# Decode attention with a gated feed-forward: one load of wo's blocks 20 to 25 in place of two, the join ahead of their rows, and ten semaphore presets on GpSimd instead of VectorE

## The chip, the cores and the metric

The kernel runs on one core of one Trainium2 chip. A core has five engines with programs of their own: TensorE (PE, with its weight loads as PEld), VectorE (DVE), ScalarE (ACT), GpSimd (POOL) and SyncE (SP), which here only issues DMA transfers. They wait for each other on semaphores. The metric is the device time of one execution in microseconds (us); lower is better. The profile is of one execution.

## The reference

One token x (512 values) goes through two branches that a scalar gate mixes. Branch A is attention with 32 query heads of 128 over a cache of 8 groups with 32,768 keys and values each; branch B is a SwiGLU feed-forward of width 1,792. All inputs are bf16.

```python
x = A_x                                              # (1, 1, 512)
g = sigmoid((x * gate_w).sum(-1, keepdims=True))
q = (x @ wq).reshape(B, Sq, 32, 128).transpose(0, 2, 1, 3)
k = repeat(k_cache, 4, axis=1); v = repeat(v_cache, 4, axis=1)   # caches (1, 8, 32768, 128)
p = softmax(einsum("bhqd,bhkd->bhqk", q, k) * 128 ** -0.5)
o = einsum("bhqk,bhkd->bhqd", p, v)
a = o.transpose(0, 2, 1, 3).reshape(B, Sq, 4096) @ wo            # wo (4096, 512)
b = (silu(x @ w_gate) * (x @ w_up)) @ w_down                     # w_down (1792, 512)
return g * a + (1 - g) * b
```

## The kernel before

The work is a stream of weights and cache through three pages of SBUF of 8 MB each (one row of 32,768 bf16 values a partition). Pages 0 and 1 take the keys of the eight groups in turn, page 2 the values, and before them wq, w_gate and w_up. Page 0 at last holds w_down and wo. All large loads stand in SP's program in one order: wq, x, gate_w, w_gate, w_up, the keys of group 0, then keys of group j+1 and values of group j by turns; a load waits on a semaphore until the page it overwrites has been read (`load_k`, L327, waits for transposes counted in `sem_tr`; `load_v`, L338, for matmuls counted in `sem_v_done`). At the end come w_down (L361), the values of the last group in three pieces (L369 to L372, each waiting for the part of the page it overwrites) and wo in six pieces (`load_wo`, L364 to L374), which wait for nothing of their own.

DVE transposes the keys piece by piece (L707), PE multiplies them with the queries (L445), DVE takes the maximum (L716), GpSimd spreads it over the partitions (L308), ACT takes exponentials (L567) and copies them into the place where PE reads them (L580), and PE multiplies them with the values (L472) and transposes the sums (L486). The loop over the groups is a real loop on PE (L534), ACT (L557) and DVE (L756).

So that the first pass needs no special case, ten semaphores get a value at the start (L605 to L611): `sem_sc`, two of `sem_v7`, `sem_v6`, `sem_k7`, `sem_acc`, `sem_red`, `sem_ep`, `sem_v` and `sem_tr`. In DVE's program these stand behind five memsets and ahead of the copy of x (L614). GpSimd's program at the start sets constants (L289 to L300), raises `sem_const` (L301) and waits for `sem_dve_gpart`, the gate's partial sums, which it adds up over the partitions (L303).

At the end the attention output (4,096 values as 32 columns `O2` of 128) meets wo, which lies as 32 blocks of 128 rows: partition p holds 32 consecutive rows of wo, 1 KB each, and block j is row j of every partition. `WO_CUTS` cuts the 32 blocks into loads, each with a semaphore of its own in `sem_wo`:

```python
WO_CUTS = [0, 16, 20, 24, 26, 30, 32]
KW = 2
KL = 4
```

The first `KW` = 2 loads (blocks 0 to 19) are multiplied in wide form (L513 to L524): a matmul per block with 512 columns, the blocks spread over four rows of `ps_w`, which already holds the feed-forward's part. DVE copies `ps_w` to `part` (L753). The rest goes in narrow form: `emit_rows` makes four matmuls of 128 columns each for a block (one for each quarter of the 512 outputs, each in a strip of 32 rows of `ps_c`), and `emit_wo(pe, k)` does so for each block of load k after a wait for `sem_wo[k]`. The join (L529) is `emit_rows` with `part` in fp32: it adds the four rows of `part` into `ps_c`. It waits for DVE's copy (`sem_dve_w`, L528).

`emit_wide` does in this order: the wide blocks; `emit_wo` of load 2 (blocks 20 to 23, L527), after a wait for `sem_dve_oz`, the spread-out copy of `O2`; the join; `emit_wo` of the loads 3 to `KL` - 1, here load 3 (blocks 24 and 25, L531). There the block "main" ends, with a barrier of all engines (L267). Behind the barrier PE does the loads from `KL` on (blocks 26 to 29, then 30 and 31), DVE casts `ps_c` to `res_row` (L767), and SP and ACT store one half each.

Of the kernel before, what the change touches and what calls it, by code (L numbers as in the profile page):

```python
# [14 lines left out]
def bass_gated_mix__gqa_block_cached__swiglu_ffn__decode_kernel(  # L15
# [31 lines left out]
    UNITS = RB // RPU  # L47
    SLOTS = 2
# [7 lines left out]
    assert S % 128 == 0 and NT == 256 and G == 8 and RB * NS * 4 == 4096  # L56
    assert KC * H * DH + 2 * KC * F <= PAGE and (FC + WOJ) * NOUT <= PAGE

    WO_CUTS = [0, 16, 20, 24, 26, 30, 32]
    KW = 2  # L60
    KL = 4
    WIDE = WO_CUTS[KW]
    RQ = 4
    NSTRIP = 4
# [12 lines left out]
    assert RQ * HPG <= 32 and RQ * DH == 512 and FC % 2 == 0  # L77
    assert WO_CUTS[-1] == WOJ and FC % 2 == 0

# [7 lines left out]
    with ExitStack() as es:  # L87
        def S_(name):
            return es.enter_context(nc.semaphore(name))
# [7 lines left out]
        sem_k7 = S_("s_k7")  # L97
        sem_v6 = S_("s_v6")
        sem_v = S_("s_v")
        sem_v7 = [sem_v] + [S_(f"s_v7{i}") for i in range(1, len(V7_CUTS) - 1)]  # L100
        sem_ld_wd = S_("s_ld_wd")
        sem_wo = [S_(f"s_wo{i}") for i in range(len(WO_CUTS) - 1)]
        sem_tr = S_("s_tr")
        sem_sc = S_("s_sc")
# [29 lines left out]
        sem_acc = S_("s_acc")  # L134
        sem_red = S_("s_red")
        sem_oc = S_("s_oc")
        sem_exp = S_("s_exp")
        sem_ep = S_("s_ep")
# [97 lines left out]
        def emit_rows(pe, lhs, rhs, last):  # L236
            for oc in range(OC):
                e = oc % RPS
                ins = pe.matmul(  # L239
                    ps_c[32 * oc : 32 * oc + (1 if e else SW), 0:128],  # L240
                    lhs(e),
                    rhs[:, oc * 128 : (oc + 1) * 128],
                    start=False,
                    stop=last,
                    skip_group_check=True,
                )
            return ins

        def emit_wo(pe, k):
            pe.wait_ge(sem_wo[k], 16)  # L250
            for j in range(WO_CUTS[k], WO_CUTS[k + 1]):
                ins = emit_rows(
                    pe,
                    lambda e: O2[:, j : j + 1] if e else O2z[:, j - WIDE, :],
                    wo_v[:, j, :],
                    j == WOJ - 1,
                )
            return ins
# [8 lines left out]
        with nc.Block("main") as block:  # L267
            @block.gpsimd
            def _(pool):
                npool = [0]  # L270

                def chain(ins):
                    ins.then_inc(sem_pool, 1)
                    npool[0] += 1
                    pool.wait_ge(sem_pool, npool[0])

                def ones_where(t, base, pattern):
                    return pool.affine_select(
                        out=t,
                        in_=t,  # L280
                        compare_op=ALU.not_equal,
                        fill=1.0,
                        base=base,
                        pattern=pattern,
                        channel_multiplier=1,
                    )

                pool.load_library(library_config.all_libraries[1])
                chain(pool.memset(eye2[:, :], 0.0))  # L289
                ones_where(eye2[:, :], 0, [[-1, 2]]).then_inc(sem_eye, 1)  # L290
                pool.memset(qblk[:, :], 0.0)
                pool.memset(spread, 0.0)
                pool.memset(ident_f[:, :], 0.0)
                pool.memset(selz[:, :], 0.0)
                chain(pool.memset(pmat[:, :], 0.0))
                ones_where(spread, 0, [[-32, NSTRIP], [0, NQ], [-1, QP]]).then_inc(sem_const, 1)
                ones_where(ident_f[:, :], 0, [[-1, 128]]).then_inc(sem_const, 1)
                ones_where(pmat[:, :], 0, [[-1, 32], [-32, 4]]).then_inc(sem_const, 1)
                for c in range(NSTRIP):
                    chain(ones_where(selz[:, SW - 1 : SW], -32 * c, [[0, 1]]))  # L300
                pool.sem_inc(sem_const, 1)  # L301
                pool.wait_ge(sem_dve_gpart, 1)
                pool.partition_all_reduce(gtot[:, :], gpart[:, :], 128, ReduceOp.add).then_inc(  # L303
                    sem_gtot, 1
                )
                for j in range(G):
                    pool.wait_ge(sem_pmax, j + 1)
                    pool.partition_all_reduce(  # L308
                        gmax[:, :], pmax[:, :], 128, ReduceOp.max
                    ).then_inc(sem_gmax, 1)  # L310
                pool.wait_ge(sem_exp, HPG * (G + 2))
                chain(pool.memset(O2z, 0.0))
                pool.partition_all_reduce(ssum[:, :], esum[:, :], 128, ReduceOp.add).then_inc(
                    sem_S, 1
                )

            @block.sync
            def _(sp):
# [45 lines left out]
                def load_wo(k):  # L364
                    a, b = WO_CUTS[k], WO_CUTS[k + 1]
                    src = A_wo.rearrange("(p j) n -> p j n", j=WOJ)
                    sp.dma_start(wo_v[:, a:b, :], src[:, a:b, :]).then_inc(sem_wo[k], 16)  # L367
# [9 lines left out]
            def _(pe):  # L377
# [129 lines left out]
                def emit_wide():  # L507
                    pe.wait_ge(sem_dve_oT2, 1)
                    pe.matmul(
                        ps_m[:, M_O0 : M_O0 + WOJ], pmat[:, :], O2a[:, :], start=True, stop=True  # L510
                    ).then_inc(sem_pe_O2, 1)
                    pe.wait_ge(sem_dve_O2, 1)
                    for k in range(KW):  # L513
                        pe.wait_ge(sem_wo[k], 16)
                        for j in range(WO_CUTS[k], WO_CUTS[k + 1]):
                            c = j % NSTRIP
                            ins = pe.matmul(
                                ps_w[32 * c : 32 * c + 1, :],
                                O2[:, j : j + 1],
                                wo_v[:, j, :],  # L520
                                start=False,
                                stop=False,
                                skip_group_check=True,
                            )  # L524
                    ins.then_inc(sem_pe_w, 1)
                    pe.wait_ge(sem_dve_oz, 1)
                    emit_wo(pe, KW)  # L527
                    pe.wait_ge(sem_dve_w, 1)  # L528
                    emit_rows(pe, lambda e: selz[:, SW - 1 : SW] if e else selz[:, :], part, False)  # L529
                    for k in range(KW + 1, KL):  # L530
                        emit_wo(pe, k)  # L531

                emit_q()
                with hinted(pe, "groups", 1, G + 3) as (p, arm):  # L534
                    arm()
                    with pe.If(((p + (G - 3)) >> 3) == 1):
                        emit_v(p - 1)
                        emit_reduce(p)
                    with pe.If(p < G + 1):
                        emit_s(p)  # L540
                    with pe.Else():
                        with pe.If(p == G + 1):
                            emit_wd()
                        with pe.Else():
                            emit_wide()
# [46 lines left out]
            def _(dve):  # L592
# [9 lines left out]
                dve.memset(ps_c[:, :], 0.0).then_inc(sem_psw, 1)  # L602
                dve.memset(ps_w[:, :], 0.0).then_inc(sem_psw, 1)
                dve.memset(ps_o[:, :], 0.0).then_inc(sem_v_done, VTURN)
                dve.sem_inc(sem_sc, SLOTS)  # L605
                for sem in sem_v7[1:] + [sem_v6, sem_k7, sem_acc]:
                    dve.sem_inc(sem, 1)
                dve.sem_inc(sem_red, 2)
                dve.sem_inc(sem_ep, 1)
                dve.sem_inc(sem_v, 16)  # L610
                dve.sem_inc(sem_tr, UNITS)  # L611
                xg = ps_m[:, M_X0 : M_X0 + 2 * KC].rearrange("p (c e) -> p e c", e=2)
                dve.wait_ge(sem_pe_x, 1)
                dve.tensor_copy(xT[:, :], xg[:, 0, :]).then_inc(sem_dve_x, 1)  # L614
# [147 lines left out]
        pe, dve = nc.tensor, nc.vector  # L762
        for k in range(KL, len(sem_wo)):
            ins = emit_wo(pe, k)
# [35 lines left out]
```

## Time and profile before

| what | value |
|---|---|
| time, median of 3 runs | 349.60 us (349.52 to 349.61) |
| time of the profiled execution | 349.47 us |
| its span (first to last instruction) | 347.9 us |
| granted TensorE clock, mean of the span | 0.619 |
| PE busy | 181.4 us, 52% |
| DVE busy | 191.2 us, 55% |
| ACT busy | 92.9 us, 27% |
| POOL busy | 8.4 us, 2% |
| bytes by DMA | 148.13 MB in 4,477 packets, mean 426 GB/s |

The page has the busy time of each engine, the span in 40 equal slices (a digit is the busy share in tenths), the DMA queues with the share of 16 DMA engines' time that their packets took, and the chain of waits that ended last. In that chain DMA holds 59% of the span, PE 18% and DVE 15%. A stretch of the chain that is put to DVE and PE in turn lies beside transfers that are still running, so a share of the chain is not by itself what an engine costs. The trace beneath the page holds every packet, every instruction and every semaphore record with its time; where a time is given to a hundredth of a microsecond below, it is from there.

### The profile page before, as it was taken

The page shows a single profiled execution, that of the slowest core. Times are in us where ns is not written, and L with a number is a line of the kernel's source. Part 1 is how long each engine was busy: PE and PEld are TensorE (multiplying, and loading weights), DVE is VectorE, ACT ScalarE, POOL GpSimd, SP SyncE. Part 2 cuts the span into 40 slices and gives each one's busy share as a digit, 9 for nine tenths or more (in the row PEclk, how much of TensorE's full clock was granted, in tenths as well). Part 3 has the DMA queues.
Part 4 walks back from the last instruction along what each step waited for, and adds up shares of the span by engine and source line. Part 5 has one row for each costly group of instructions (what it writes and reads, how often), then busy time and mean ns, then how long its engine had stood idle before and what let it go on. Part 6 is the DMA issues. An engine that isn't in the chain of part 4 may idle for free.

```text
span 347.9 us, 7702 instructions
## 1 busy us (share of the span) xinstructions
PE 181.4 (52%) x2755; PEld 110.9 (32%) x2755; DVE 191.2 (55%) x311; ACT 92.9 (27%) x220; POOL 8.4 (2%) x29
## 2 busy tenths in 40 slices
PE   0393553556426570556235570556245575567555
PEld 0141442443124420443124420443034334431112
DVE  4024996996059911995069802994079839920001
ACT  1002002902640057003810057003810075038000
POOL 4000000000000000000000000000000000010000
PEclk9998555555855566555855567555855585558655
DMA  8999999989899898998989989899898999999996
GB/s 332 415 460 422 482 392 452 482 362 482 362 482 482 362 482 362 482 482 362 482 362 482 482 362 482 362 482 475 369 482 362 422 463 441 422 407 467 392 428 268
DMA packets 4477, 148.13 MB, mean 426 GB/s; under 512 B 506, under 2 KB 508, under 8 KB 1148
## 3 DMA queue, kind: packets, MB, share of 16 engines
q1 hardware_dynamic: 4472, 148.12, 98.9%
q8 instruction: 1, 0.02, 0.0%
q10 hardware_dynamic: 4, 0.00, 0.0%
HBM read 148.11 MB, written 0.00 MB: 426 GB/s over the span
## 4 chain that ended last, share of the span: by engine, by line
DMA 59%; PE 18%; DVE 15%; issue 7%; SPq 1%; DVEq 0%
DMA page<-in_A_k_cache_dram 39%; DVE slot L707 13%; DMA page<-in_A_wo_dram 8%; DMA page<-in_A_v_cache_dram 8%; PE ps_sc L445 7%; PE ps_o L472 5%; PE ps_sc L400 4%; DMA E<-in_gate_w_dram 3%; SPq L367 0%; SPq L320 0%; DVE qblk L637 0%; PE ps_c L239 0%; DVE E L654 0%; DVE oT L695 0%; DVE E L663 0%
## 5 line engine op out<-in xcount | busy, mean ns | idle before, releaser
L707 DVE STREAM_TRANSPOSE slot<-page 128x512 f32<-128x512 f32 x256 | 167.0, 690 | 91.2 <-DMA page<-in_A_k_cache_dram 81.1
L445 PE MATMUL ps_sc<-qcur,slot 128*128 128x16 bf16 x2048 | 103.6, 179 | 123.4 <-DVE slot L707 110.0
L445 PEld LDWEIGHTS ps_sc<-qcur,slot 128*128 128x128 bf16 x2048 | 81.0, 107 | 147.0 <-issue 146.4
L472 PE MATMUL ps_o<-page,ET 128*16 128x512 bf16 x512 | 45.4, 529 | 16.9 <-issue 10.4
L580 ACT ACTIVATE ET<-E 32x256 bf16<-32x256 bf16 x128 | 52.8, 412 | 1.4
L562 ACT ACTIVATE nbias<-gmax 128x4 f32<-128x4 f32 x8 | 1.6, 206 | 182.6 <-POOL gmax L308 182.6
L472 PEld LDWEIGHTS ps_o<-page,ET 128*16 128x16 bf16 x512 | 15.9, 114 | 42.9 <-issue 34.4
L567 ACT ACTIVATE E<-ps_sc,nbias 128x256 bf16 x32 | 21.8, 848 | 1.8 <-ACT nbias L562 1.8
L400 PE MATMUL ps_sc<-page,slot 128*128 x64 | 14.9, 399 | 1.0 <-DVE prod_col L618 1.0
L739 DVE TENSOR_REDUCE oT<-ps_o 128x4 f32<-128x64 f32 x1 | 0.2, 224 | 22.9 <-PE ps_o L486 22.9
L716 DVE TENSOR_REDUCE pmax<-ps_sc 128x4 f32<-128x1024 f32 x8 | 9.8, 1226 | 4.7 <-PE ps_sc L445 4.7
L562 ACT ACT_TABLE_LOAD x8 | 10.3, 1283 | 0.1
L308 POOL PARTITION_ALL_REDUCE gmax<-pmax x8 | 3.0, 373 | 290.6 <-DVE pmax L716 290.6
L400 PEld LDWEIGHTS ps_sc<-page,slot 128*128 x64 | 6.7, 105 | 8.8 <-issue 3.3
L567 ACT ACTIVATION_READ_ACCUMULATOR E<-ps_sc,nbias x32 | 9.1, 284 | 0.0
L576 ACT ACTIVATE acc<-ps_o 128x512 f32<-128x512 f32 x8 | 4.8, 606 | 15.3 <-PE ps_o L472 15.3
L486 PE MATMUL ps_o<-ident_f,acc 128*128 128x128 f32 x32 | 5.7, 305 | 5.6 <-ACT acc L576 4.9
L498 PE MATMUL ps_w<-page,vec 128*1 x14 | 6.4, 470 | 2.4 <-DMA page<-in_B_w_down_dram 1.4
L383 PE MATMUL ps_m<-eye,E 2*128 2x2 bf16 x4 | 0.3, 166 | 13.0 <-DMA E<-in_gate_w_dram 13.0
L486 PEld LDWEIGHTS ps_o<-ident_f,acc 128*128 128x128 f32 x32 | 3.7, 150 | 10.0 <-ACT acc L576 8.4
L627 DVE CAST E<-ps_sc 128x1024 bf16<-128x1024 f32 x1 | 1.2, 1225 | 9.3 <-PE ps_sc L400 9.3
L589 ACT ACTIVATE acc<-ps_o 128x512 f32<-128x512 f32 x1 | 0.6, 598 | 15.8 <-PE ps_o L472 15.8
(63 smaller groups left out, 35.1 us busy)
## 6 DMA issues: line engine op xcount, KB each, us to landing
page<-in_A_k_cache_dram SPq DMA_DIRECT2D x4, 4096.0 KB, 37.5
page<-in_A_v_cache_dram SPq DMA_DIRECT2D x3, 4096.0 KB, 19.2
page<-in_A_wq_dram SPq DMA_DIRECT2D x1, 4096.0 KB, 12.1
page<-in_A_v_cache_dram SPq DMA_DIRECT2D x1, 3072.0 KB, 19.8
page<-in_A_wo_dram SPq DMA_DIRECT2D x1, 2048.0 KB, 26.3
page<-in_B_w_gate_dram SPq DMA_DIRECT2D x1, 1792.0 KB, 15.3
page<-in_B_w_up_dram SPq DMA_DIRECT2D x1, 1792.0 KB, 19.2
page<-in_B_w_down_dram SPq DMA_DIRECT2D x1, 1792.0 KB, 32.3
```

What stands on the lines that cost most here:

```text
L308: pool.partition_all_reduce(gmax[:, :], pmax[:, :], 128, ReduceOp.max).then_inc(sem_gmax, 1)
L400: ins = pe.matmul(ps_sc[:, ps(i) * 512 : ps(i) * 512 + width], slot[:, bass.ds(x[i % NSTRIP], 128)], page[:, bass.ds(w[i], width)], start= ...
L445: ins = pe.matmul(ps_sc[:, bass.ds(c0 + u * (SLOTS * RPU * NS) + (s * RPU + r) * NS, NS),], sv[:, s, r, e // 2, e % 2, :], qcur[:, e, :], ...
L472: ins = pe.matmul(ps_o[32 * c : 32 * c + VW, :], ET[:, k * VW : (k + 1) * VW], rows(V_PAGE, n, n + RQ), start=(k < NSTRIP), stop=(k >= NT ...
L486: ins = pe.transpose(ps_o[:, q * 128 : (q + 1) * 128], acc[:, q * 128 : (q + 1) * 128], ident_f[:, :],)
L498: pe.matmul(ps_w[0:1, :], vec[:, bass.ds(n, 1)], page[:, bass.ds(n * NOUT + o0, NOUT)], start=False, stop=False, skip_group_check=True,)
L562: act.activation(nbias[:, :], gmax[:, :], ACT.Copy, scale=-SCALE).then_inc(sem_nbias, 1)
L567: act.activation(ev[:, h, :, :], scv[:, h, :, :], ACT.Exp, bias=nbias[:, h : h + 1], scale=SCALE, accum_out=esum[:, bass.ds(j * HPG + h, 1 ...
L576: act.activation(acc[:, :], ps_o[:, :], ACT.Copy).then_inc(sem_acc, 1)
L580: ins = act.activation(etv[QP * i : QP * (i + 1), :, g, :], E[QP * g : QP * (g + 1), i * w : (i + 1) * w].rearrange("p (f m) -> p f m", f=KH),
L707: dve.transpose(slot_f[:, s * (SLOT // 2) : (s + 1) * (SLOT // 2)].rearrange("p (x g b) -> p g x b", g=NQ, b=QP), kp[:, f, :, tu * UW : (t ...
L716: dve.tensor_reduce(pmax[:, :], ps_sc[:, p * RB * NS : (p + 1) * RB * NS].rearrange("p (x h) -> p h x", h=HPG), AX.X, ALU.max,).then_inc(s ...
```

## The change

Loads 2 and 3 of wo (blocks 20 to 23, blocks 24 and 25) become one load of six blocks, so there are five loads of wo and five semaphores `sem_wo`, and `KL` is 3. `emit_wo(pe, KW)` ahead of the join goes away, and the loop behind the join starts at `KW`: the join now stands ahead of the rows of blocks 20 to 25, which are all behind it. The ten presets leave DVE's program and stand in GpSimd's between the last constant and the wait for the gate's partial sums.

```diff
-    WO_CUTS = [0, 16, 20, 24, 26, 30, 32]
+    WO_CUTS = [0, 16, 20, 26, 30, 32]
     KW = 2
-    KL = 4
+    KL = 3
...
                 pool.sem_inc(sem_const, 1)
+                pool.sem_inc(sem_sc, SLOTS)
+                for sem in sem_v7[1:] + [sem_v6, sem_k7, sem_acc]:
+                    pool.sem_inc(sem, 1)
+                pool.sem_inc(sem_red, 2)
+                pool.sem_inc(sem_ep, 1)
+                pool.sem_inc(sem_v, 16)
+                pool.sem_inc(sem_tr, UNITS)
                 pool.wait_ge(sem_dve_gpart, 1)
...
                     pe.wait_ge(sem_dve_oz, 1)
-                    emit_wo(pe, KW)
                     pe.wait_ge(sem_dve_w, 1)
                     emit_rows(pe, lambda e: selz[:, SW - 1 : SW] if e else selz[:, :], part, False)
-                    for k in range(KW + 1, KL):
+                    for k in range(KW, KL):
                         emit_wo(pe, k)
...
                 dve.memset(ps_o[:, :], 0.0).then_inc(sem_v_done, VTURN)
-                dve.sem_inc(sem_sc, SLOTS)
-                for sem in sem_v7[1:] + [sem_v6, sem_k7, sem_acc]:
-                    dve.sem_inc(sem, 1)
-                dve.sem_inc(sem_red, 2)
-                dve.sem_inc(sem_ep, 1)
-                dve.sem_inc(sem_v, 16)
-                dve.sem_inc(sem_tr, UNITS)
                 xg = ps_m[:, M_X0 : M_X0 + 2 * KC].rearrange("p (c e) -> p e c", e=2)
```

## The prediction

> **What bounds the kernel now.** I read the core line first (span 347.9 us, mean granted clock 0.619), then the page's second and third parts, then stretches of the span, then the end and the start of the span in order of time.
>
> ```profile
> DMA  8999999989899898998989989899898999999996
> GB/s 332 415 460 422 482 392 452 482 362 482 362 482 482 362 482 362 482 482 362 482 362 482 482 362 482 362 482 475 369 482 362 422 463 441 422 407 467 392 428 268
> ...
> q1 hardware_dynamic: 4472, 148.12, 98.9%
> q8 instruction: 1, 0.02, 0.0%
> ```
>
> The DMA engines' packets fill 98.9% of sixteen spans, while PE and DVE are busy about half of it. The stretches say the same without the coarse slices:
>
> ```profile
> core 0: us, PE busy (x) PEld busy (x) DVE busy (x) ACT busy (x) POOL busy (x), PEclk, DMA share, GB/s
> ...
> 300.00:345.30 45.30, 28.64 (x289) 10.68 (x291) 9.05 (x20) 10.58 (x27) 1.33 (x3) 0.61 1.00 422
> 345.30:347.90 2.60, 0.91 (x24) 0.37 (x18) 0.29 (x1) 0.00 (x0) 0.00 (x0) 0.50 0.03 7
> ```
>
> The share is 1.00 until 345.3 us. In the trace's packet records the first data packet starts at 1.74 us, no microsecond between 3 and 345 has fewer than 15.8 of the 16 engines at work, and the last block of wo is reported landed at 345.77 us. So the time is: 1.57 us outside the span (349.47 of the profiled execution less 347.9), 1.74 before the stream, 344.03 of stream, and 2.14 behind it. An edit counts only if it shortens the packets, opens a hole in the stream, or alters those 2.14 us. Holes are far off:
>
> ```profile
> 311.32 2.95 SPq L320 DMA_DIRECT2D page<-in_A_v_cache_dram  x3
> ...
> 314.31 4.67 SPq L367 DMA_DIRECT2D page<-in_A_wo_dram  x6
> ```
>
> The V load issued at 311.32 finds w_down still in transfer until 316.21 (its landing record), 4.9 us of stock, the thinnest that I found; the older loads keep 8 us and more. The six loads of wo are issued by 319 us and begin to land at 340.62.
>
> The end, in order of time (start, duration, then in brackets the idle time before and its releaser):
>
> ```profile
> 343.11 0.69 DVE L753 COPY acc<-ps_w 128x512 f32<-128x512 f32 x1 [2.92 <-PE ps_w L517]
> ...
> 343.33 0.27 PE L239 MATMUL ps_c<-page,slot 128*32 128x128 bf16 x1 [0.27 <-DMA page<-in_A_wo_dram]
> ...
> 343.86 0.20 PEld L239 LDWEIGHTS ps_c<-acc,selz 128*32 128x32 f32 x8 [0.18 <-DVE acc L753]
> 343.86 0.65 PE L239 MATMUL ps_c<-acc,selz 128*32 128x128 f32 x8
> ...
> 345.19 0.29 PE L239 MATMUL ps_c<-page,slot 128*32 128x128 bf16 x1 [0.47 <-DMA page<-in_A_wo_dram]
> ...
> 345.81 0.10 PEld L239 LDWEIGHTS ps_c<-page,slot 128*32 128x32 bf16 x1 [0.28 <-DMA page<-in_A_wo_dram]
> ...
> 346.27 0.29 DVE L767 CAST res_row<-ps_c 128x128 bf16<-128x128 f32 x1 [2.47 <-PE ps_c L239]
> ```
>
> Blocks 20 to 23 run at 343.33, the join at 343.86 behind DVE's copy, 24 and 25 behind it; then PE idles 0.47 us, runs 26 to 29 at 345.19 when they land, and 30, 31 at 345.81. That 0.47 us is the cover the change spends.
>
> **The change, part by part.** *The merged load.* Before, a partition gets a 4,096-byte packet for blocks 20 to 23 and a 2,048-byte one for 24 and 25; after, one of 6,144. Median packets last 84 ns (2,048 bytes), 162 (4,096) and 313 (8,192). The last two give 37 ns for each further 1,024 bytes, so 6,144 bytes are estimated at 162 + 75 = 237. An engine carries 8 partitions: 8 x (162 + 84 - 237) = 72 ns less, and one 4-byte semaphore packet of 9 ns less: 0.08 us. The landings agree: 343.19, 343.86, 345.15, 345.77 are 0.67, 1.29 and 0.62 us apart, so 2 x (0.62 to 0.67) - 1.29 = -0.05 to 0.05 us goes with a load as such. I take 0.08 and keep -0.05 as the other end. The merged load lands at 343.86 - 0.08 = 343.78, 26 to 29 at 345.07, 30 and 31 at 345.69. SP issues five loads instead of six, 0.43 us less (a row of L367), at 316 us, 24 us before their bytes arrive: nothing.
>
> By the Trainium skill ("DMA: Bandwidth & Descriptors", "Anatomy of one DMA") a DMA has a fixed part of about 2 us, which speaks for more gain than this; on the path it describes, from GpSimd. Loads here land 0.62 us apart, so that part is overlapped with the neighbours; the sum by it would be 347.6.
>
> *The order on PE.* The join can't start before DVE's copy ends (343.81), as now: 343.86. Its eight passes occupy PE until the next rows start at 344.25 in this trace (0.39 us). Until then PE idles where blocks 20 to 23 stood. Behind the join now come six blocks instead of two, all landed. A block is four matmuls side by side; successive blocks start 0.107 us apart (343.39, 343.50, 343.61 in the timeline of PE). So the sixth starts at 344.25 + 5 x 0.107 = 344.78, its last matmul 0.055 later, and with 0.314 for that matmul the end is 345.15, against 344.72 now: 4 x 0.107 = 0.43 later.
>
> Queued behind is the barrier at the end of the block "main" (L267), at which all engines wait for PE. The trace's semaphore records show PE's drain end 0.03 us after the last matmul, GpSimd's gather and release, and PE past it at 344.975, 0.25 us after its last matmul. So now 345.40, later than the landing of 26 to 29 (345.07): this wait replaces the DMA's. Rows follow an expired wait within 0.025 to 0.04 us (343.27 to 343.30 ahead of block 20), so blocks 26 to 29 start at 345.44 instead of 345.19. Four blocks later, 345.44 + 4 x 0.1 = 345.83, PE is ready for 30 and 31, which are there since 345.69; in the trace of before they start at 345.815. From there two blocks back to back and DVE's start take 0.46 (345.815 to 346.27) to 0.50: the cast starts at 346.29 to 346.34.
>
> Bounds: if rows behind the barrier start as fast as a first block does (0.065 us to the next, not 0.107) and the chain holds no other delay, the landing decides again and all 0.08 comes through. If the first row behind the barrier needs as long as the 0.22 us between 344.975 and 345.19 (most of which was waiting for the data), 0.18 us more. I take +0.04, between 346.29 and 346.34, with -0.08 and +0.22 as ends.
>
> *The presets.* On DVE they are ten semaphore instructions from 0.915 to 1.77 us, 0.093 apart, while its memsets run, which end at 5.15.
>
> ```profile
> 13.31 0.16 DVE L614 CAST xT<-ps_m 128x4 bf16<-128x4 f32 x1 [8.16 <-PE ps_m L383]
> ...
> 13.96 0.40 POOL L303 PARTITION_ALL_REDUCE gtot<-gpart  x1 [8.51 <-DVE gpart L622]
> ```
>
> DVE then idles 8.16 us for x and gate_w: removing 0.93 us there gains nothing. GpSimd passes its last preset now at 5.50; ten more at the same spacing end at 6.4, with its 8.51 us idle as cover. The first reader is DVE's transpose at 34.42. Without cover it would be 0.93 us on GpSimd's reduction at 13.96, whose reader on ACT waits for PE until 29.20 anyway. Cost 0.
>
> **Sum.** 349.47 + 0.04 = 349.51 for an execution like the profiled one. The median shown lies 0.13 higher (349.60), so 349.64, said as 349.6. A measurement of this kernel can tell about 0.2%, 0.7 us, from no change: this is no change.
>
> **Rivals.** *PE keeps its cover* (0.26): all the lower bounds hold, the landing ends the chain, 349.60 - 0.08 = 349.5. For it: the margin is only 0.1 us at 30 and 31. Against: the 0.107 spacing is steady in every run of blocks.
>
> *The load as such is dear* (0.04): a load leaves the stream idle at its end and merging removes that. The most that could go is the whole step of a two-block load, 0.67 us: 348.9. Against: the step is 8 packets x 84 ns = 0.67, so nothing is idle. It would be the answer of the skill's rule above.
>
> *A code fetch moves onto the path* (0.06), the slower side. The page counts one instruction packet; in the records it has 16,384 bytes, starts at 346.09 and takes 0.98 us, while the last rows drain. DVE's program becomes ten instructions shorter and GpSimd's ten longer, so another piece of code may end at a boundary. Exposed once, it costs its 0.98: 350.6. It decides only for code needed after 345.77; earlier, the 4.9 us of stock hides it. Against: DVE's loop and PE's whole program ran without any fetch in the span. The Trainium skill ("Runtime: NRT & Kernel Launch", "Instruction fetch mechanics") says that code comes in blocks of 16 KiB, as that one packet agrees, and that crossing a boundary is mostly hidden.
>
> *The six blocks do not run abreast* (0.02): with one matmul per 0.107 us instead of four, 24 take 2.57 instead of 0.64: 351.5. Against: both runs of four blocks in this trace go four at a time.
>
> *The change does nothing it says*: for the presets that is my forecast. It has no time of its own.
>
> **How the numbers follow.** Forecast 0.62, covered 0.26, dear load 0.04, fetch 0.06, serial rows 0.02. The first two lie within 0.2%: same 0.88, faster 0.04, slower 0.08. The unknown costs run from 349.5 to 349.8; the three runs and the profiled one differ by 0.14, and another chip or day may add as much again; reaching towards both rivals without taking in their whole price, 349.2 to 350.2.
>
> **What would show it.** The queue row should read 4,328 packets (128 data and 16 semaphore packets fewer) and the same bytes. The join should start at about 343.86 with no block rows ahead of it, 24 matmuls follow without a wait for DMA, and the idle before 26 to 29 be put down to the barrier or vanish; the cast at 346.2 to 346.5. POOL's and DVE's rows at 13 us should stand still. I am wrong if the DMA share falls under 0.99 in any stretch before 345, if the last landing moves by over 0.2 us, if instruction packets appear ahead of 345, or if the cast starts after 346.6.

## The result and the profile after

The changed kernel takes 353.30 us (median of 5 executions, 352.62 to 353.33) against 349.61 us (349.52 to 349.73) for the kernel before: ratio 1.0101, interval 1.0086 to 1.0116. It is slower by 3.7 us, and the span hardly shows it: 348.5 us in the profiled execution, 348.4 to 348.6 in all five. The time that the program's instructions do not cover went from 1.57 us to 4.12 us in the profiled execution (352.62 - 348.5) and to 4.6 to 4.9 us in the other four. Spans of the kernel before, in later series beside the experiments, have a median of 348.0 to 348.1. So some 0.4 us lie within the span and some 3.3 us behind it.

The DMA queues on the page of the changed kernel (packets, MB, share of 16 engines' span):

```profile
q1 hardware_dynamic: 4328, 148.12, 98.7%
q14 instruction: 1, 0.01, 0.0%
```

The loads are as forecast: 4,328 packets, the same bytes. The other row is the finding. Before, there was a packet of queue 8 in the span, 16 KB of instructions at 346.09 us; now there is none, and instead one of queue 14, 8 KB. The packet records beneath the page, all instruction packets of at least 8 KB from 0 us on (queue, start, us, bytes):

```
kernel    span    instruction packets                       time outside the span
before    347.9   q8 346.09 0.98 16384                      1.57
changed   348.5   q14 316.74 0.31 8192, q8 350.52 0.93 16384  4.12
```

The packet of queue 8 is not gone. It comes 2.0 us behind the end of the span, where no instruction of the kernel runs. The trace also has semaphore records behind the span: the steps of two barriers with a reset of the semaphores between them. In the kernel before the last step stands at 349.35, within 0.2 us of the execution's time (349.47), so times behind the span can be set against that time. In the changed kernel the last recorded step stands at 350.23; then come the packet, 350.52 to 351.45, and some 1.2 us more until the execution is over at 352.62. Of the 2.55 us by which 4.12 exceeds 1.57, 2.27 lie behind that last step (2.39 against 0.12) and 0.29 before it.

The end of the span, PE and DVE in order of time:

```profile
343.54 0.69 DVE L752 COPY acc<-ps_w 128x512 f32<-128x512 f32 x1 [2.92 <-PE ps_w L524]
...
344.38 0.65 PE L239 MATMUL ps_c<-acc,selz 128*32 128x128 f32 x8 [0.89 <-DVE acc L752]
...
345.95 0.10 PEld L239 LDWEIGHTS ps_c<-page,slot 128*32 128x32 bf16 x1 [0.55 <-DMA page<-in_A_wo_dram]
345.98 0.26 PE L239 MATMUL ps_c<-page,slot 128*32 128x128 bf16 x1 [0.31 <-PEq L267]
...
346.85 0.29 DVE L766 CAST res_row<-ps_c 128x128 bf16<-128x128 f32 x1 [2.62 <-PE ps_c L239]
```

The join now leads, six blocks follow it without a wait, and the matmuls behind the barrier wait for `PEq L267`, the barrier itself, as the prediction had it. The row of their weight load still names the DMA, but that load is reported landed at 345.49, and the barrier was passed at 345.92. All of it is later than forecast, because DVE's copy starts at 343.54 instead of 343.11: the last piece of the values is reported landed at 336.14 instead of 335.72. A load is reported landed sixteen times, and here the last report is alone: the fifteenth stands at 335.85 (before: 335.68 and 335.72). w_down, ahead of the packet of queue 14, shows no such gap (316.30 and 316.35). So some 0.3 us of the delay came behind that packet, on one of sixteen parts of the stream.

The start is as it was. The presets on GpSimd are past at 6.27 us; the row of the reduction counts them as idle time, and 7.7 us of it are left behind them:

```profile
13.31 0.16 DVE L613 CAST xT<-ps_m 128x4 bf16<-128x4 f32 x1 [8.17 <-PE ps_m L390]
...
13.96 0.40 POOL L310 PARTITION_ALL_REDUCE gtot<-gpart  x1 [8.52 <-DVE gpart L621]
```

### The profile page after: what moved, and what is told of

It is laid out like the page before. It is cut to its first block, busy times and chain, and to the rows that moved or that the text cites. A ratio compares the mean times of both kernels' runs of the same rounds, so it can differ in the third digit from the quotient of the medians.

```text
span 348.5 us, 7701 instructions
## 1 busy us (share of the span) xinstructions
PE 183.1 (53%) x2755; PEld 111.8 (32%) x2755; DVE 191.2 (55%) x311; ACT 92.9 (27%) x220; POOL 8.3 (2%) x29
## 3 DMA queue, kind: packets, MB, share of 16 engines
q1 hardware_dynamic: 4328, 148.12, 98.7%
## 5 line engine op out<-in xcount | busy, mean ns | idle before, releaser
L479 PE MATMUL ps_o<-page,ET 128*16 128x512 bf16 x512 | 46.8, 542 | 17.2 <-issue 10.4
```

The lines of the kernel that those rows point to most:

```text
L479: ins = pe.matmul(ps_o[32 * c : 32 * c + VW, :], ET[:, k * VW : (k + 1) * VW], rows(V_PAGE, n, n + RQ), start=(k < NSTRIP), stop=(k >= NT ...
```

## The experiments

An execution is called long where over 3.8 us lie outside its span, and short where it is under 1.9. Of the kernel before, none of 108 executions beside the experiments was long.

**Which part of the change.** `e1_cuts_only` is the changed kernel with the presets back on VectorE, `e2_presets_only` the kernel before with the presets on GpSimd.

The first, against the changed kernel:

```diff
                 pool.sem_inc(sem_const, 1)
-                pool.sem_inc(sem_sc, SLOTS)
...
-                pool.sem_inc(sem_tr, UNITS)
...
                 dve.memset(ps_o[:, :], 0.0).then_inc(sem_v_done, VTURN)
+                dve.sem_inc(sem_sc, SLOTS)
...
+                dve.sem_inc(sem_tr, UNITS)
```

> The five loads of wo and the join ahead of blocks 20 to 25 as in the changed kernel, the presets back on VectorE. Theory A (the moved presets shift code, and a code fetch lands behind the span): the time outside the span is back at 1.6 us, no instruction packet at 316 us, time 349.6 to 349.8 with the cast 0.05 to 0.15 us later than 346.27. Theory B (the loads and the join are the cause): time 352.6 to 353.3, outside the span 4 to 5 us.

Measured: 349.79 to 350.00 us in five executions and 352.36 to 353.39 in the other five; spans 348.1 to 348.5 in both sorts, 1.5 to 1.7 us outside or 4.1 to 4.9. Each theory described half of the executions. The order and the load together suffice for long executions, but not in every one.

The second, against the kernel before, is the same move the other way:

```diff
+                pool.sem_inc(sem_sc, SLOTS)
...
-                dve.sem_inc(sem_sc, SLOTS)
...
```

> Presets on GpSimd, six loads of wo and the old order. Theory A: time 352.4 to 353.3, outside the span 4 to 5 us, an instruction packet near 316.7 us and one of 16 KB behind the end. Theory B: 349.6, as before the change.

Measured: 349.92 us (349.62 to 350.19, ten executions) against 349.58; ratio 1.0009, interval 1.0000 to 1.0019. No long execution: theory A has fallen for the 3.3 us. There is an 8 KB packet in the span, and the median span is 348.35 against 348.0. The 0.3 us stand at the edge of what this series can tell from nothing.

**GpSimd longer or VectorE shorter.**

In `e3_pool_long` GpSimd gets ten idle increments and VectorE keeps its presets; in `e4_dve_short` the presets stand at the start of ScalarE's program. Both against the kernel before:

```diff
                 pool.sem_inc(sem_const, 1)
+                for _ in range(10):
+                    pool.sem_inc(sem_pad, 1)
```

> The kernel before with ten more semaphore instructions in GpSimd's program (on a semaphore that nobody reads) and VectorE's program as it was. If GpSimd's longer program moves the fetch: 352.4 to 353.3 with 4 to 5 us outside the span. If VectorE's shorter program does it: 349.6, as before.

```diff
                 act.sem_inc(sem_exp, 2 * HPG)
+                act.sem_inc(sem_sc, SLOTS)
...
-                dve.sem_inc(sem_sc, SLOTS)
...
```

> The kernel before with the ten presets on ScalarE, so VectorE's program is ten shorter and GpSimd's as it was. If VectorE's shorter program moves the fetch: 352.4 to 353.3. If GpSimd's longer one did it: 349.6, unless ScalarE's ten more do the same in its place, which the instruction packets' times would show.

Measured: 349.88 us (349.53 to 350.06) and 350.02 us (349.76 to 350.36), ratios 1.0009 and 1.0010, no long execution in ten each, so neither causes the 3.3 us. The small loss follows the engine that got longer. In e3 the 8 KB packet starts at 317.85, 3.9 us after GpSimd's drain at the end of its block has ended; in e2 and in the changed kernel 3.4 and 3.5 us after it. In e4 it starts at 341.06, 3.0 us after ScalarE's drain. No kernel with the programs of both GpSimd and ScalarE as before has such a packet. Ten instructions more bring a fetch of code behind the drain, through the full stream of loads; that a block's boundary has moved there is what the packets suggest.

**The load or the order.** In `e5_five_old_order` the six blocks of the merged load run ahead of the join; in `e6_six_join_first` there are six loads as before and only the order changes. `e7_barrier_early` is the changed kernel with its narrow blocks all behind the barrier, `e8_before_barrier_early` the same with six loads and the presets on VectorE.

Against the kernel before, e5:

```diff
-    WO_CUTS = [0, 16, 20, 24, 26, 30, 32]
+    WO_CUTS = [0, 16, 20, 26, 30, 32]
-    KL = 4
+    KL = 3
```

> Five loads of wo as in the changed kernel, but blocks 20 to 25 ahead of the join as in the old order, and the presets on VectorE. Theory L (one load fewer is the cause of the 3 us outside the span: SP is through with its loads at 317 us instead of 319): some or all executions at 352.4 to 353.4 with over 4 us outside the span. Theory O (the order on PE, which reaches the barrier of the block 0.7 us later, is the cause): 349.5 to 349.9, outside 1.6 us.

e6, against the kernel before:

```diff
                     pe.wait_ge(sem_dve_oz, 1)
-                    emit_wo(pe, KW)
                     pe.wait_ge(sem_dve_w, 1)
...
-                    for k in range(KW + 1, KL):
+                    for k in range(KW, KL):
```

> Six loads of wo as before, the join ahead of blocks 20 to 25, the presets on VectorE. Theory L: 349.6 to 349.9 in every execution, outside 1.6 us. Theory O: some or all executions at 352.4 to 353.4.

e7, against the changed kernel; e8 is e6 with `KL = 2` in place of 4:

```diff
-    KL = 3
+    KL = 2
```

> The changed kernel with KL = 2: all narrow blocks stand behind the barrier of the block, which PE reaches right after the join, about 0.6 us earlier. Theory O: the fetch is early again, outside 1.6 us, time 349.6 to 350.0. Theory L: as the changed kernel, 352.6 to 353.3.

> The kernel before with KL = 2 and the join ahead of blocks 20 to 25, which so stand behind the barrier; six loads, presets on VectorE. Theory O: at most 349.6, the cast up to 0.1 us earlier if the barrier held PE up. Theory L: the same; six loads stay.

Measured: e5 has four long of five (352.38 to 353.12, and 350.02), e6 four long of six (352.35 to 353.35, and 349.67, 349.78). e7 has none of ten: 350.08 us (349.86 to 350.31), ratio 1.0016, interval 1.0006 to 1.0025. e8 none of ten: 349.75 us, ratio 1.0005. The merged load is not needed for long executions (e6), and taking only the barrier forward cures the changed kernel: 353.3 to 350.1 by one constant. Both pages count 7,701 instructions, so no program has become longer or shorter by it. Theory L has fallen, but the load is not innocent: in e5 the old order does not help, since the six blocks now wait for one load and the join stands behind them. PE passes the barrier at 345.88 us, as in the changed kernel (345.92; before: 344.98), in e6 at 345.51. The merged load alone (e5) and the new order alone (e6) each bring a late barrier, and each brings long executions.

In e7 the queue row is back on the page, and PE passes the barrier at 345.34:

```profile
q8 instruction: 1, 0.02, 0.0%
q14 instruction: 1, 0.01, 0.0%
```

and in order of time:

```profile
344.43 0.65 PE L239 MATMUL ps_c<-acc,selz 128*32 128x128 f32 x8 [0.89 <-DVE acc L752]
345.37 0.10 PEld L239 LDWEIGHTS ps_c<-page,slot 128*32 128x32 bf16 x1 [0.74 <-issue]
345.40 0.27 PE L239 MATMUL ps_c<-page,slot 128*32 128x128 bf16 x1 [0.32 <-PEq L267]
```

Join, barrier, and all twelve narrow blocks behind it.

**What about the barrier counts, and whose code it is.** `e9_late_end` puts work between the last matmul and the cast, `e10_before_barrier_late` moves the barrier of the kernel before and nothing else, `e11_pe_pad` lengthens PE's program at its start, `e12_five_barrier_early` joins the merged load with an early barrier and the presets on VectorE.

e9, against the changed kernel:

```diff
+        dve.memset(acc[:, :], 0.0)
         dve.tensor_copy(res_row[:, :], ps_c[:, 0:128]).then_inc(sem_dve_row, 1)
```

> The changed kernel with a memset of acc (128 x 512 fp32) on VectorE between the last matmul and the cast of the result, about 0.48 us more work on the path behind the barrier. Theory T (what counts is the time from the barrier of the block to the end: a code fetch is asked for at the barrier, 2.6 us are too short for it and 3.0 are enough): the longer kernel becomes FASTER, 350.3 to 350.7, outside 1.6 us, the 16 KB packet within the span. Theory S (what counts is the barrier's place against the end of the stream of loads): 353.1 to 353.8, outside 4 to 5 us.

e10, against the kernel before:

```diff
-    KL = 4
+    KL = 5
```

> The kernel before with KL = 5: blocks 26 to 29 stand ahead of the barrier too, only 30 and 31 behind it. Nothing else differs. Theory T and theory S: the barrier passes at 345.9 or later, 2.3 us ahead of the end, so 352.4 to 353.5 with over 4 us outside in all executions. Theory C (the changed code itself, not the barrier's time): 349.6 to 350.0.

e11, against the changed kernel; e12 is e1 with `KL = 2`:

```diff
                 def emit_q():
+                    for _ in range(64):
+                        pe.sem_inc(sem_pad, 1)
                     pe.wait_ge(sem_eye, 1)
```

> The changed kernel with 64 semaphore instructions more at the start of PE's program, while PE waits for x. If the 16 KB packet is PE's code: its boundary comes 64 instructions earlier, the packet moves to before 345 us or into the early part of the span, and the time is 349.9 to 350.4. If it is another engine's: 352.6 to 353.3 as the changed kernel.

> Five loads, the join first, KL = 2 and the presets on VectorE: the merged load without the late barrier and without the longer program of GpSimd. All theories: 349.4 to 349.8, outside 1.5 us, no 8 KB packet within the span; the merged load's 0.08 us could show as much below the run with six loads and KL = 2 (349.75).

Measured: e9 three long of six (353.30 to 353.78; short 350.43 to 350.73): the time from barrier to end (theory T) does not decide by itself, and neither does the barrier's place against the stream (theory S), by which all would be long. In e4, too, PE passed the barrier at 345.65 in the profiled execution, later than in e6, and none of ten was long. e10 three long of ten (352.63 to 353.58; short 349.58 to 350.18): the barrier's place alone makes long executions of the kernel before, but fewer than either theory asked for.

e11 is the clearest: no long execution of seven, 350.82 us (350.55 to 351.40), and on its page:

```profile
q8 instruction: 2, 0.03, 0.0%
q14 instruction: 2, 0.01, 0.0%
```

PE's program alone grew, and queue 8 has a second packet of 16 KB, at 34.04 us, some 4 us after PE entered the first pass over the groups (29.8 to 30.2). So queue 8 carries PE's code. The packet takes 1.04 us in the stream of loads, and the stream does not make it up: of the sixteen reports for w_down the fifteenth stands at 316.39, the last at 317.46 us (316.2 to 316.6 in the other kernels). The median span is 349.4, 1 us longer than the changed kernel's. e12: 349.81 us (349.41 to 350.44), ratio 1.0007, interval 0.9997 to 1.0016, none long; the merged load's 0.08 us can't be seen against e8's 349.75.

**Where PE's next block of code is missed.** `e13_pe_waits_row` and `e16_cuts_pe_waits` let PE wait at its end, `e14_pe_one_start` is the control for the moved code, `e15_changed_again` the changed kernel on the same chip.

The wait, against the changed kernel (e13) and against e1 (e16); e14 has one `pe.sem_inc(sem_pad, 1)` where e11 has 64:

```diff
         dve.tensor_copy(res_row[:, :], ps_c[:, 0:128]).then_inc(sem_dve_row, 1)
+        pe.wait_ge(sem_dve_row, 1)
```

> The changed kernel with one instruction more: at its end PE waits for the cast of the result (sem_dve_row), so it leaves its program about 0.6 us later, and nothing on the path to the stores waits for it. Theory P (PE's next block of code is asked for when PE passes the barrier, and is missed if PE runs from the barrier to the end of its program in under 0.6 us; where it took 0.9 us or more no execution was long): 349.9 to 350.3 in every execution, outside 1.5 us. If PE's time behind the barrier is not it: over half of the executions at 352.5 to 353.5.

> The control for it: the changed kernel with one PE instruction more at the start of its program, so the code behind has the same new place as with the wait, and the end runs as in the changed kernel. Theory P: as the changed kernel, most or all executions at 352.5 to 353.5. If the code's place is the cause: 349.9 to 350.3.

> The changed kernel as it is, on the same chip as the other three: how often it is long. All theories: 352.5 to 353.5 in over half of the executions; some may come out near 350.0.

> Merged load and join first with the presets on VectorE, and PE waiting for the cast at its end. Theory P: no execution is long; 349.7 to 350.0, that is the merged load and the order on PE cost 0.1 to 0.4 us by themselves. Otherwise about half at 352.4 to 353.4, as without the wait.

Measured: e13 nine long of twelve, e14 five of five, e15 four of four, e16 eight of twelve. Theory P has fallen: a wait at PE's end does not bring the block in time. All four profiled executions are long, and in them the packet of queue 8 starts at 349.78 to 350.66. In e13, e14 and e16 the semaphore records behind the span show what waits: of nine steps of the last barrier, eight are through at 349.98 (e13) and the ninth comes at 352.63, after the packet. In all three it comes 1.4 to 1.5 us after the packet's end.

The last pair, against the changed kernel: `e17_pe_eight_after` has eight instructions behind the barrier, `e18_pe_eight_start` the same eight where e11 has 64.

```diff
+        for _ in range(8):
+            pe.sem_inc(sem_pad, 1)
         for k in range(KL, len(sem_wo)):
             ins = emit_wo(pe, k)
```

> The changed kernel with eight semaphore instructions on PE right behind the barrier, ahead of blocks 26 to 29: PE takes 0.4 to 0.8 us longer from the barrier to its last matmul, and the path to the stores grows by as much. Theory Q (the next block of PE's code is missed when PE runs through its rows behind the barrier in under 0.6 us, as all kernels with long executions do, and not when it takes 0.9 us or more): 350.4 to 350.9 in every execution, outside 1.5 us: more work and a shorter time. Otherwise over half of the executions at 353.0 to 354.0.

> The control: the same eight instructions at the start of PE's program, where PE waits for x; the code behind has the same place as in the other kernel, and PE's time behind the barrier is the changed kernel's. Theory Q: 352.5 to 353.5 in most or all executions. If the place of the code is the cause: 349.9 to 350.3.

Measured: e18, the control, 350.96 to 351.27 us in five executions, 2.5 to 2.8 us outside, a value that no kernel had before; its packet starts at 347.05, 0.57 us after PE's last matmul begins, and the reset of the semaphores behind the span ends at 350.81 instead of 349.36. The first of the two barriers, whose first step stands at 347.00 in the changed kernel, begins only at 349.88, 1.5 us after the packet's end (e17: 350.81 and 1.6 us). So here the end waits for the same block one barrier earlier. e17: two executions with 1.5 us outside (351.25, 351.32) and four with 2.4 to 3.0 (352.19 to 352.89). Theory Q has fallen as stated, and so has its rival: eight instructions at either place in PE's program move the point at which the block is needed. The two short executions of e17 against none of e18 suggest that the time behind the barrier has a say too, which is not shown.

## Why the prediction was wrong

*The stream.* The packets were forecast rightly: those of 6,144 bytes last 239 ns in the median (forecast 237). The merged load lands 1.91 us after the one before it (344.22 less 342.31), where the two loads took 1.28 + 0.67 = 1.95, so 0.04 of the forecast 0.08 us shows. That the stream as a whole would stay where it was is what failed: the last landing is at 346.11 instead of 345.77.

*The order on PE.* Right in mechanism: the join led, the barrier replaced the load as the releaser. The barrier was passed at 345.92 instead of 345.40, of which 0.43 us is DVE's copy, late by the end of the values; the cast came at 346.85 instead of 346.29 to 346.34. What the order and the merged load cost apart from presets and long executions stays open: the five short executions of e1 have a median of 349.87 against 349.58, but the four of e16, with one wait more on PE, 349.49 against 349.64.

*The presets.* "Cost 0" was wrong by some 0.3 us (e2; e3 has as much). The working looked at when the instructions run, where there is cover of 8 us. What it missed is that a program that gets longer moves what lies behind it: GpSimd's code behind its drain came in an extra 8 KB packet through a stream without a gap. The packet took 0.31 us, and in the changed kernel one of the sixteen parts of the stream is behind by some 0.3 us from there on. It costs time only where that part is the last to land: in the trace of e2 another part was behind already (fifteenth and last report 316.27 and 316.44 ahead of the packet, 326.16 and 326.18 behind it). One trace doesn't prove it, for e16 has a step of 0.25 us at the same place without such a packet; the median spans of e2, e3 and e4, 348.35 to 348.4 against 348.0, speak for it.

*The step that failed* is in the first part: "So the time is: 1.57 us outside the span (349.47 of the profiled execution less 347.9)", and with it "An edit counts only if it shortens the packets, opens a hole in the stream, or alters those 2.14 us." The 1.57 us was taken as a constant. It is one only as long as PE's next 16 KB of code comes within the span (at 346.09 in the kernel before); in every long execution that was profiled the packet comes behind the span, the end waits for it, and 1.57 becomes 4 to 5. What does it is the later barrier on PE, 0.9 us later in the changed kernel: the order alone brings long executions (e6), so does the merged load alone (e5), so does the barrier's place alone (e10), and an early barrier cures the changed kernel (e7). The presets alone bring none (e2).

*The rival "A code fetch moves onto the path"* named the thing and the point from which it decides, code needed after 345.77, and the very packet. It failed in three points: a chance of 0.06, a price of 0.98 us (the packet's own duration) where the measured one is 3.3, and the cause, which it sought in the programs of DVE and GpSimd. The price was too small because the packet's duration is only part of the delay: in the changed kernel it starts 0.29 us after the last step of the final barrier and is followed by 1.2 us more. Two of its arguments were wrong as well. "PE's whole program ran without any fetch in the span": the packet at 346.09 was PE's (e11). And "earlier, the 4.9 us of stock hides it": the stock keeps the loads coming, but in a full stream a packet of code takes time of its own, 0.3 us (e2) or 1 us (e11). Of the Trainium skill's sentence ("Runtime: NRT & Kernel Launch", "Instruction fetch mechanics") that crossing a block boundary is mostly hidden, the trace agrees for the kernel before and contradicts it for the changed one: 3.3 us are not hidden.

*The rivals "The load as such is dear" and "The six blocks do not run abreast"* did not happen: the landing steps above, and six blocks 0.107 us apart from 344.77 to 345.30.

*The signs that the prediction set* were good: an instruction packet ahead of 345 (316.74), a last landing over 0.2 us later (346.11 after 345.77) and a cast after 346.6 (346.85) all came. But they point at the 0.4 us within the span; none looked behind it.

*What stays open.* What decides whether PE's block is asked for in time. Shown are the packets, whose code it is (e11), and that the barrier's place alone produces long executions (e10) and an early barrier none (e7, e8, e12: 0 of 30). In all kernels without long executions and with PE's program as it was, PE spent 0.92 us or more from the barrier to its last matmul; with long ones 0.58 or less (e10: 0.14). That this time is the cause is only argued: e13, e16 and e17 tried to lengthen PE's end in two ways and did not settle it, and e10, with the shortest time, was long in only three of ten. The traces add when the packet comes: 0.6 to 1.5 us after PE passed the barrier in the short profiled executions of these kernels, 3.9 to 4.7 us after it in the long ones. No kernel was profiled in both sorts; the nearest pair is e1 (short, 346.73) and e16 (long, 350.66), one wait apart. Nor is it shown that the presets raise the rate, though with them 9 of 9 executions of the changed kernel were long and without them (e1) 5 of 10.

No version beats the kernel before: the best without a long execution are e8 (349.75) and e12 (349.81), both the same as 349.55 to 349.57 within their intervals.

## What to carry to other kernels

Compare the measured time with the span before summing an edit: what lies outside belongs to the program too, and an edit to PE's last microseconds lengthened it here by 3.3 us, where the span grew by 0.4. Read the rows of instruction packets as part of the profile: where they stand in the span, whose code they are, and what moves if that engine's program grows by a few instructions or ends later. In this stream of loads without gaps each packet of code had a price, also one for an engine that was idle.

## What the runs showed of the hardware

The same program, unchanged, had two times that are 3 us apart, with equal spans (e1: 348.1 to 348.5 in both sorts); the profiled executions put this down to when one 16 KB block of PE's code arrives. One instruction packet of 16 KB amid the loads cost about 1 us of span (e11), one of 8 KB some 0.3 us (e2, e3). When the end waited for the block, the next step came 1.4 to 1.6 us after the packet's end (e13, e14, e16, e17, e18). And a memset that put the cast 0.5 us further back made three of six executions shorter than any of the changed kernel (e9: 350.43 to 350.73 against 352.57 to 353.33).
